# The end of an attention-plus-mixer kernel: last exponentials read from the PSUM banks, values by key tile, softmax sums spread by a matrix product instead of transposed, branch hints on four engines

## The chip, the cores and the metric

One core of one Trainium2 chip runs the whole program. The metric is the device time of one execution in microseconds (us); the median of three runs of the kernel before is 927.33 us (925.99 to 928.0). Engines: PE (TensorE), DVE (VectorE), ACT (ScalarE), POOL (GpSimd) and SP (SyncE, which here issues DMAs and closes the program).

## The reference

The input is one sequence of 2048 tokens with 448 channels. The output mixes two branches with a gate per token: `g * a + (1 - g) * b`, g being the sigmoid of `(x * gate_w).sum(-1)`.

```python
def _A_ref(x, wq, wk, wv, wo):                  # a: 16 query heads of 28, one shared key/value head
    q = (x @ wq).reshape(B, S, H, Dh).transpose(0, 2, 1, 3)
    k = x @ wk
    v = x @ wv
    scores = jnp.einsum("bhqd,bkd->bhqk", q, k) * (Dh ** -0.5)
    p = _softmax(scores, axis=-1)
    o = jnp.einsum("bhqk,bkd->bhqd", p, v)
    return o.transpose(0, 2, 1, 3).reshape(B, S, H * Dh) @ wo
```

Branch b (layer norm, a shifted token mixer, an MLP of width 1792) is finished before the part that this case is about.

## The kernel before, in words

The first 400 us or so project, split matrices into high and low parts, and run branch b; the last 500 us are attention. Attention is 16 units `u` (4 token blocks of 512 by 4 groups of 4 heads), and every unit has 8 stretches `v` of two key tiles of 128 keys each. In a stretch PE makes the scores of 4 heads for two key tiles (L831: three products for each head, into four PSUM banks); `exps` turns a bank into exponentials. Of the four heads, three banks are read by ACT directly (L855, 128x512 each). The fourth (`DRAIN`, head 3) is first copied to SBUF by DVE (L852), and ACT takes both key tiles' copies in one 128x1024 instruction (L860, `late_exps`). The read order of the heads is 0, 3, 1, 2. One stretch later `values` (L871) multiplies the exponentials by `vext`, which holds a column of ones and the 28 value channels: row 32j of the result for head j is the softmax sum. Values go by half of the 512 queries (256 columns), inside a half by key tile; a half's result is added to `o` (128 x 512, L876).

When a unit is done, its sums are fetched from `o` by a small DMA (`sums_begin`, tile `rt`), tested against a limit (`check`, tile `good`), inverted, and sent through DRAM to be spread over 32 partitions (`recip`, tile `rb`); `norm` multiplies, and `wo_job` (L793) multiplies by the output projection, four products side by side in four column groups. DVE then adds the gated result to `ot` (L801), and the output goes out by DMA.

The last unit has no later unit to hide this. Its end before the change is written out (L916 to L996): the sums are added to `o` in four 128x128 pieces (L963), PE transposes `o` (L968) so that the sums lie along the free axis, DVE inverts 8 columns of sums at a time (L931) and multiplies (L935), PE transposes back (L940), ACT copies to SBUF (L941), PE projects (L793), DVE (L951; for token tile 1 ACT L948 and POOL L949) gates and adds, and four DMAs store (L953). Between them `keep_warm` issues bf16 products that nobody reads (L960). The test of the sums ends in one number, `redo`, made from `worst` (L982, then PE L989, DVE L992 and L993). All five engines load `redo` into a register (L996) and branch: if a sum was out of bounds a second, exact pass over all of attention follows (`tc.If`, some thousands of instructions); otherwise they jump over it to the closing instructions (L1071). In the profiled execution the jump is taken. On PE alone `mark_branch_hint_location` puts a hint instruction for that jump in front of the end.

All engines' orders are written by hand (`manual_schedule`): each engine runs its rows in program order, and an instruction that waits holds all that stand behind it on its engine.

## Time and profile before

| what | us |
|---|---|
| median of the runs (3), lowest, highest | 927.33, 925.99, 928.0 |
| the profiled execution | 926.66 |
| its span, first to last instruction | 924.7 |
| PE, ACT, DVE, POOL busy in the span | 911.7, 634.5, 542.2, 104.2 |
| last matmul of the program ends, after about | 917.6 |
| last DVE instruction ends, after about | 918.4 |

Times inside the span count from its first instruction. The 2.0 us between the span and the execution's time lie around the program. Rows of the trace are read as: start, duration, engine, line, operation, written tile <- read tiles, shapes, count, and in brackets the idle time before and what ended it. An engine name with q (SPq, DVEq) is that engine's sequencer: waits, register loads, branches, DMA issues.

### The profile page before, as it was taken

What the parts mean: (1) busy time and instruction counts of PE and PEld (TensorE: products, weight loads), DVE (VectorE), ACT (ScalarE), POOL (GpSimd) and SP (SyncE); (2) the same over time, 40 slices, a digit from 0 to 9 for tenths busy, and PEclk for the clock granted to TensorE, in tenths of its full rate; (3) what the DMA queues carried; (4) which work ended last, traced back from release to release, by engine and by line L of the source; (5) the groups of instructions that cost most, each with busy time, mean ns of one, the idle gap of its engine ahead of it and who ended that gap; (6) DMA issues with size and microseconds to landing.
All of it is one profiled execution on the core that took longest, in us unless ns stands there. A gap on an engine that the chain in (4) does not pass through costs nothing.

```text
span 924.7 us, 23960 instructions
## 1 busy us (share of the span) xinstructions
PE 911.7 (99%) x10051; PEld 647.5 (70%) x10051; DVE 542.2 (59%) x1081; ACT 634.5 (69%) x1134; POOL 104.2 (11%) x135
## 2 busy tenths in 40 slices
PE   9999999999999999999999999999999999999996
PEld 6788888888888888875566666666655656666663
DVE  4665263631435736446666666666666666666664
ACT  5542434432231232259999999999999999999993
POOL 2233200212000440031000000000000000000000
PEclk9999999999999999999999999999999999999999
DMA  9801534130122042110000001001011100110001
GB/s 303 300 27 26 169 128 129 22 84 21 33 65 60 19 104 61 38 54 23 25 23 6 26 14 53 26 26 26 8 41 46 26 4 24 35 45 3 14 14 44
DMA packets 40691, 50.72 MB, mean 55 GB/s; under 512 B 8752, under 2 KB 26880, under 8 KB 40576
## 3 DMA queue, kind: packets, MB, share of 16 engines
q1 hardware_dynamic: 37552, 43.65, 16.4%
q10 hardware_dynamic: 3024, 5.47, 1.6%
q8 instruction: 80, 1.31, 0.6%
q14 instruction: 35, 0.29, 0.1%
HBM read 37.04 MB, written 11.93 MB: 53 GB/s over the span
## 4 chain that ended last, share of the span: by engine, by line
PE 93%; ACT 3%; DMA 2%; DVE 1%; issue 0%; SPq 0%; DVEq 0%; ACTq 0%
PE bank L871 23%; PE bank L831 21%; PE bank L793 7%; PE acc L655 5%; PE acc L654 5%; PE acc L656 5%; PE g L132 4%; PE g L131 4%; PE g L133 4%; ACT p L855 2%; DMA xkv<-in_xT_dram 2%; PE hs L437 1%; PE hs L436 1%; PE hs L438 1%; PE g L135 1%; PE g L134 1%
## 5 line engine op out<-in xcount | busy, mean ns | idle before, releaser
L855 ACT ACTIVATE p<-bank 128x512 f32<-128x512 f32 x768 | 391.0, 626 | 5.8 <-PE bank L831 5.8
L871 PE MATMUL bank<-p,vext 128*32 128x256 f32 x3072 | 243.9, 379 | 2.1 <-ACT p L855 2.1
L871 PE MATMUL bank<-pd,vext 128*32 128x256 f32 x1024 | 242.2, 379 | 0.3 <-ACT pd L860 0.3
L852 DVE COPY pd<-bank 128x512 f32<-128x512 f32 x256 | 176.6, 691 | 53.2 <-PE bank L831 52.3
L871 PEld LDWEIGHTS bank<-p,vext 128*32 128x32 f32 x3072 | 125.1, 110 | 85.8 <-ACT p L855 5.1
L644 ACT ACTIVATE gh<-g 128x512 fp32r<-128x512 f32 x55 | 32.8, 597 | 189.5 <-PE g L135 189.5
L876 DVE TENSOR_TENSOR o<-o,bank 128x256 f32<-128x256 f32 x222 | 93.5, 421 | 91.3 <-ACT p L855 51.0
L860 ACT ACTIVATE pd<-pd 128x1024 f32<-128x1024 f32 x128 | 143.0, 1117 | 0.0
L831 PE MATMUL bank<-qh,kH 30*128 30x512 f32 x1024 | 119.6, 443 | 0.0
L871 PEld LDWEIGHTS bank<-pd,vext 128*32 128x32 f32 x1024 | 111.6, 110 | 1.3 <-ACT pd L860 0.7
L646 DVE TENSOR_TENSOR gl<-gf,gh 128x512 fp32r<-128x512 f32 x55 | 37.9, 690 | 125.5 <-ACT gf L645 125.4
L831 PE MATMUL bank<-qh,kL 28*128 28x512 f32 x1024 | 106.2, 394 | 0.0
L831 PE MATMUL bank<-ql,kH 28*128 28x512 f32 x1024 | 105.7, 389 | 0.0
L831 PEld LDWEIGHTS bank<-qh,kH 30*128 30x128 f32 x1024 | 60.9, 182 | 58.4 <-ACT p L855 47.0
L655 PE MATMUL acc<-w4l,gh 128*128 128x448 f32 x220 | 80.4, 366 | 0.0
L654 PE MATMUL acc<-w4h,gh 128*128 128x448 f32 x220 | 80.3, 365 | 0.0
L656 PE MATMUL acc<-w4h,gl 128*128 128x448 f32 x220 | 80.1, 364 | 0.0
L793 PE MATMUL bank<-wof,on 128*32 128x224 f32 (+1 forms) x992 | 73.1, 370 | 0.3 <-ACT p L855 0.3
L132 PE MATMUL g<-al,w3h 128*128 128x512 f32 x168 | 65.8, 392 | 0.0
L131 PE MATMUL g<-ah,w3h 128*128 128x512 f32 x168 | 65.6, 390 | 0.0
L133 PE MATMUL g<-ah,w3l 128*128 128x512 f32 x168 | 65.5, 390 | 0.0
L831 PEld LDWEIGHTS bank<-ql,kH 28*128 28x128 f32 x1024 | 52.6, 185 | 8.3
(196 smaller groups left out, 1164.8 us busy)
## 6 DMA issues: line engine op xcount, KB each, us to landing
qd<-qf ACTq DMA_DIRECT2D x16, 256.0 KB
qm<-qd SPq DMA_DIRECT2D x16, 256.0 KB
qr<-qd SPq DMA_DIRECT2D x16, 256.0 KB
rb<-rd SPq DMA_DIRECT2D x15, 256.0 KB
x<-in_x_dram SPq DMA_DIRECT2D x4, 896.0 KB
xd<-xt SPq DMA_DIRECT2D x16, 224.0 KB
w34raw<-in_w_dram SPq DMA_DIRECT2D x7, 512.0 KB
out_dram<-ot SPq DMA_DIRECT2D x15, 224.0 KB
```

Of the source, the lines that this page charges most:

```text
L131: nc.tensor.matmul(ps, wh[:, c, :], ah[:, c, :], start=(c == 0), stop=False)
L132: nc.tensor.matmul(ps, wh[:, c, :], al[:, c, :], start=False, stop=False)
L133: nc.tensor.matmul(ps, wl[:, c, :], ah[:, c, :], start=False, stop=False)
L654: nc.tensor.matmul(ps, gh[:, tok], w4h[i][:, k, :], start=(f == 0), stop=False)
L655: nc.tensor.matmul(ps, gh[:, tok], w4l[i][:, k, :], start=False, stop=False)
L656: nc.tensor.matmul(ps, gl[:, tok], w4h[i][:, k, :], start=False, stop=(f == stop))
L793: nc.tensor.matmul(ps[32 * j:32 * j + 32, cols], on_of[u][:, tok], wof[:, g, cols], start=True, stop=True, tile_position=(0, 32 * j))
L831: nc.tensor.matmul(bs[j], w, a, start=(i == 0), stop=(i == 2), tile_position=(32 * j, 0))
L852: nc.vector.tensor_copy(ps[j], bs[j])
L855: behind[kt % 2] = nc.scalar.activation(ps[j], bs[j], AF.Exp, scale=SCALE)
L860: ins = nc.scalar.activation(pd, pd, AF.Exp, scale=SCALE)
L871: nc.tensor.matmul(pv[32 * j:32 * j + 32, q], vext[:, kt, :], p_of[u, kt][j][:, q], start=(kt % 2 == 0), stop=(kt % 2 == 1), tile_position ...
```

## The change

In words:

- The last stretch (`last`) no longer copies head 3's banks; ACT reads all eight banks of the two key tiles, and there is no `late_exps`.
- The last values go by key tile, both halves of key tile 14 and then both of 15; two adds of 128x256 replace four of 128x128.
- The sums are spread by PE: `spread` is a 128x128 matrix whose row 32j holds ones in columns 32j to 32j+31, so that `spread` times `o` puts head j's sum on all its 32 partitions. DVE inverts this result over all columns (128, 128 and 256 of them) and multiplies `o` by it. The transpositions, ACT's copies and the POOL add are gone.
- The test of the last sums goes back to `rt`, fetched by DMA, and stands behind token tile 1's output on DVE. `redo` is now made after the last output instead of before the last two.
- Token tile 3 is projected and stored in two halves of 224 channels. Odd tiles are stored from ACT's queue, even ones from SP's.
- `keep_warm` is called for 2 products in all, instead of 5, 3, 2 and 2.
- The hint stands on PE, DVE, ACT and SP instead of PE alone.
- `spread` is filled by POOL ahead of the attention loop (five memsets).

```diff
-        def exps(u, kt, bs):
+        def exps(u, kt, bs, drain=True):
...
-                if j == DRAIN:
+                if drain and j == DRAIN:
...
+        def value(u, kt, i, pv):
+            q = HALVES[i]
+            for j in range(4):
+                nc.tensor.matmul(pv[32 * j:32 * j + 32, q], vext[:, kt, :], p_of[u, kt][j][:, q],
+                                 start=(kt % 2 == 0), stop=(kt % 2 == 1), tile_position=(0, 32 * j))
...
+            last = k == NU * NV - 1
             for kt in (2 * v, 2 * v + 1):
-                exps(u, kt, scores(u, kt))
-            late_exps(u, v)
+                exps(u, kt, scores(u, kt), not last)
+            if not last:
+                late_exps(u, v)
...
+        pvs = [take(), take()]
+        for kt in (NT - 2, NT - 1):
+            for i in range(2):
+                value(u, kt, i, pvs[i])
+        for i, q in enumerate(HALVES):
+            nc.vector.tensor_add(o[:, q], o[:, q], pvs[i][:, q])
...
+        def spread_sums(i):
+            nc.tensor.matmul(bc[i][:, HALVES[i]], spread, o[:, HALVES[i]], start=True, stop=True)
...
+        def divide(a, b):
+            nc.vector.reciprocal(rb[:, a:b], bc[a // 256][:, a:b])
+            nc.vector.tensor_mul(on_of[u][:, a:b], o[:, a:b], rb[:, a:b])
+
+        def store(n, cols):
+            queue = nc.scalar if n % 2 else nc.sync
+            queue.dma_start(out[0, n * P:(n + 1) * P, cols], ot_of[n][:, cols])
+
+        keep_warm(2)
         with tc.block():
-            tc.mark_branch_hint_location("redo", "LikelyTaken", [mybir.EngineType.PE])
-            keep_warm(5)
-            for t in range(4):
-                nc.tensor.transpose(tp[t // 2][:, t % 2], o[:, toks[t]], ident)
-        keep_warm(3)
-        tail_sums(0)
...
+            tc.mark_branch_hint_location("redo", "LikelyTaken", [
+                mybir.EngineType.PE, mybir.EngineType.DVE, mybir.EngineType.Activation, mybir.EngineType.SP])
+            spread_sums(0)
+        _, _, rt = sums_begin(u, o)
+        spread_sums(1)
+        divide(0, 128)
+        divide(128, 256)
+        divide(256, 512)
+        for t in range(3):
+            wo_job(u, t, send=store)
+            if t == 1:
+                check(rt)
+                worst = s3.tile([P, 1], F32, name="worst")
+                nc.vector.tensor_reduce(worst, good, axis=AX.XY, op=ALU.min)
+        for h in range(2):
+            wo_job(u, 3, slice(224 * h, 224 * h + 224), store)
+        tw = sent[0:1, 0:P]
         nc.tensor.transpose(tw, worst, ident)
         least = s3.tile([1, 1], F32, name="least")
         redo = s3.tile([1, 1], mybir.dt.int32, name="redo")
         nc.vector.tensor_reduce(least, tw, axis=AX.X, op=ALU.min)
         nc.vector.tensor_scalar(redo, least, -1.0, 1.0, op0=ALU.mult, op1=ALU.add)
-        tail_wo(2)
-        tail_wo(3)
         again = nc.values_load(redo, min_val=0, max_val=1)
```

What DVE runs between its last adds to `o` and the load of `redo`, before (line, operation, written tile <- read tiles, columns; numbers behind names are buffers):

```order
L931 RECIPROCAL rr_10955<-bank_3478 128x8
L935 TENSOR_TENSOR on_10956<-bank_3478,rr_10955 128x128 x2
L763 SCALAR_TENSOR_TENSOR good<-bank_3483,good 128x8
L763 SCALAR_TENSOR_TENSOR good<-bank_3478,good 128x8
L982 TENSOR_REDUCE worst<-good 128x1
L951 SCALAR_TENSOR_TENSOR ot_9803<-bank_3483,gg,ot_9803 128x448
L992 TENSOR_REDUCE least<-bank_3481 1x1
L993 TENSOR_SCALAR redo<-least 1x1
L951 SCALAR_TENSOR_TENSOR ot_10033<-bank_3484,gg,ot_10033 128x448
L951 SCALAR_TENSOR_TENSOR ot_10156<-bank_3479,gg,ot_10156 128x448
L996 TENSOR_LOAD redo
```

And the same place of DVE now, from the last reciprocal on (the two ahead of it, with their products, have 128 columns each):

```order
L946 RECIPROCAL rb_10962<-bank_3484 128x256
L947 TENSOR_TENSOR on_10961<-o_10560,rb_10962 128x256
L802 SCALAR_TENSOR_TENSOR ot_9809<-bank_3479,gg,ot_9809 128x448
L802 SCALAR_TENSOR_TENSOR ot_9926<-bank_3482,gg,ot_9926 128x448
L766 SCALAR_TENSOR_TENSOR good<-rt_10971,good 128x16
L968 TENSOR_REDUCE worst<-good 128x1
L802 SCALAR_TENSOR_TENSOR ot_10039<-bank_3485,gg,ot_10039 128x448
L802 SCALAR_TENSOR_TENSOR ot_10162<-bank_3480,gg,ot_10162 128x224
L802 SCALAR_TENSOR_TENSOR ot_10162<-bank_3483,gg,ot_10162 128x224
L975 TENSOR_REDUCE least<-bank_3478 1x1
L976 TENSOR_SCALAR redo<-least 1x1
L977 TENSOR_LOAD redo
```

All four token tiles' outputs now stand behind the last reciprocal, and `redo` has moved from between the outputs to the very end.

What ACT runs from its last two exponentials to the branch, before:

```order
L855 ACTIVATE p_3505<-bank_3478 128x512
L860 ACTIVATE pd_3513<-pd_3513 128x1024
L964 UNCONDITIONAL_BRANCH x2
L941 COPY on_10954<-bank_3481 128x128
L941 COPY on_10954<-bank_3484 128x128
L941 COPY on_10954<-bank_3479 128x128
L941 COPY on_10954<-bank_3482 128x128
L948 ACTIVATE y<-bank_3478,gg 128x448
L953 DMA out_dram<-ot_9920 128x448
L996 TENSOR_LOAD redo
L999 COMPARE_AND_BRANCH
```

And now:

```order
L858 ACTIVATE p_3512<-bank_3483 128x512
L858 ACTIVATE p_3513<-bank_3478 128x512
L954 UNCONDITIONAL_BRANCH
L1052 BRANCH_PREFETCH_HINT
L954 UNCONDITIONAL_BRANCH
L951 DMA out_dram<-ot_9926 128x448
L951 DMA out_dram<-ot_10162 128x224 x2
L977 TENSOR_LOAD redo
L980 COMPARE_AND_BRANCH
```

ACT has two 128x512 exponentials in place of one 128x1024, then only a hint and three DMA issues up to the branch; DVE and SP have the same hint at the same place of the program.

More of the change, by code (lines that the diff above doesn't have):

```diff
@@ L756, in gated_mix_kernel, with check @@
         on_of = {}
-        good = s3.tile([P, 8, 4], F32, name="good")
+        good = s3.tile([P, 4, 4], F32, name="good")
         nc.gpsimd.memset(good, 1.0)
-        def check(sums, c):
-            g = good[:, c:c + sums.shape[1]]
-            nc.vector.scalar_tensor_tensor(g, sums, LIMIT, g, op0=ALU.is_le, op1=ALU.min)
+        spread = s3.tile([P, P], F32, name="spread")
+        nc.gpsimd.memset(spread, 0.0)
+        for j in range(4):
+            nc.gpsimd.memset(spread[32 * j:32 * j + 1, 32 * j:32 * j + 32], 1.0)
+        def check(rt):
+            nc.vector.scalar_tensor_tensor(good, rt.rearrange("p (a b) -> p a b", b=4), LIMIT, good,
+                                           op0=ALU.is_le, op1=ALU.min)
         def sums_begin(u, o):
@@ L785, in gated_mix_kernel, with wo_job @@
         ot_of = {}
-        def wo_job(u, t, end=None, cols=slice(0, D)):
+        def wo_job(u, t, cols=slice(0, D), send=None):
             b, g = divmod(u, NG)
```

97 lines of the change are left out of this document (23 added, 74 removed).

## The prediction

> **What bounds the kernel now.** I read the page first, for whether any engine but PE matters.
>
> ```profile
> span 924.7 us, 23960 instructions
> PE 911.7 (99%) x10051; PEld 647.5 (70%) x10051; DVE 542.2 (59%) x1081; ACT 634.5 (69%) x1134; POOL 104.2 (11%) x135
> ```
>
> PE is busy almost throughout, and the change leaves its 900 us of loops as they are. POOL's five extra memsets stand ahead of the attention loop on an engine that is busy for 11%; behind them it weighs four tiles that PE's fifth stretch needs, so four stretches hide them, and they would cost some tenths if not. The question is the last 20 us. The chain of waits, asked for that stretch (start, duration, what), ends with the last output add:
>
> ```profile
> 902.31 1.73 PE bank L871 x32
> ...
> 908.02 0.94 ACT pd L860
> ...
> 909.01 1.91 PE bank L871 x26
> ...
> 917.69 0.68 DVE ot L951
> ```
>
> That is at 918.4, and the span ends at 924.7: 6.3 us are neither matmul nor vector work. The branch to the end and its closing lines fill them (durations in ns, then first and last start in us):
>
> ```profile
> L999 SPq EVENT_SEMAPHORE  x8: 17/17/17, 922.8 to 923.3; - x8
> L999 POOLq COMPARE_BRANCH  x1: 45/45/45, 917.1 to 917.1; - x1
> L999 PEldq COMPARE_BRANCH  x1: 998/998/998, 917.1 to 917.1; - x1
> L999 POOLq EVENT_SEMAPHORE  x1: 17/17/17, 917.7 to 917.7; - x1
> L999 PEldq EVENT_SEMAPHORE  x1: 51/51/51, 918.2 to 918.2; - x1
> L999 DVEq COMPARE_BRANCH  x1: 72/72/72, 918.4 to 918.4; - x1
> L999 ACTq COMPARE_BRANCH  x1: 54/54/54, 918.7 to 918.7; - x1
> L999 SPq COMPARE_BRANCH  x1: 45/45/45, 919.9 to 919.9; - x1
> L999 DVEq EVENT_SEMAPHORE  x1: 21/21/21, 922.2 to 922.2; - x1
> L999 ACTq EVENT_SEMAPHORE  x1: 17/17/17, 922.6 to 922.6; - x1
> ```
>
> ```profile
> L1071 PEldq BRANCH_PREFETCH_HINT  x1: 45/45/45, 909.1 to 909.1; - x1
> ```
>
> From its branch to its next instruction PE, the one engine with a hint, needs 1.1 us and POOL 0.6, but DVE 3.8, ACT 3.9 and SP 2.9. SP is last, and from there its closing waits take 1.9 us to the end of the span (922.8 to 924.7). A table by stretches shows what runs meanwhile (last three columns: granted PE clock, share of the DMA engines, GB/s), and the DMA view from 917.6 on counts the packets that carry instructions (packets, MB, share):
>
> ```profile
> 918.50:920.40 1.90, 0.00 (x0) 0.00 (x0) 0.00 (x0) 0.00 (x0) 0.00 (x0) 1.00 0.98 353
> 920.40:922.30 1.90, 0.00 (x0) 0.00 (x0) 0.00 (x0) 0.00 (x0) 0.00 (x0) 1.00 0.11 31
> ```
>
> ```profile
> q14 instruction: 6, 0.05, 2.2%
> q8 instruction: 1, 0.02, 1.0%
> ```
>
> The outputs fill the DMA engines until 920.4; a remainder drips on until 922.3, beside some of seven instruction fetches. So **two things end at nearly the same time**: SP's branch (922.8) and the last output (about 922.3).
>
> **The change, term by term.** Durations first (busy us, mean ns of one):
>
> ```profile
> L774 DVE RECIPROCAL rr<-rt 128x16 f32<-128x16 f32 x15 | 3.7, 246 | 0.0
> L763 DVE SCALAR_TENSOR_TENSOR good<-rt,good 128x16 f32<-128x16 f32 x15 | 2.5, 166 | 0.0
> ```
>
> ```profile
> L876 DVE TENSOR_TENSOR o<-o,bank 128x256 f32<-128x256 f32 x5 | 2.1, 421 | 2.1 <-PE bank L871 1.3 <-ACT p L855 0.8
> L951 DVE SCALAR_TENSOR_TENSOR ot<-bank,gg,ot 128x448 f32<-128x448 f32 x3 | 2.1, 684 | 1.5 <-PE bank L793 1.5
> L801 DVE SCALAR_TENSOR_TENSOR ot<-bank,gg,ot 128x224 f32<-128x224 f32 x4 | 1.6, 441 | 0.0
> L935 DVE TENSOR_TENSOR on<-bank,rr 128x128 f32<-128x128 f32 x4 | 1.0, 286 | 0.1
> L931 DVE RECIPROCAL rr<-bank 128x8 f32<-128x8 f32 x2 | 0.4, 204 | 0.5 <-PE bank L968 0.5
> L992 DVE TENSOR_REDUCE least<-bank 1x1 f32<-1x128 f32 x1 | 0.3, 279 | 0.7 <-PE bank L989 0.7
> L763 DVE SCALAR_TENSOR_TENSOR good<-bank,good 128x8 f32<-128x8 f32 x2 | 0.2, 156 | 0.0
> ```
>
> ```profile
> 904.98 3.04 ACT L855 ACTIVATE p<-bank 128x512 f32<-128x512 f32 x6 [0.30 <-PE bank L831]
> ```
>
> ```profile
> 911.90 0.21 DVE L931 RECIPROCAL rr<-bank 128x8 f32<-128x8 f32 x1 [0.45 <-PE bank L968]
> 912.14 0.49 DVE L935 TENSOR_TENSOR on<-bank,rr 128x128 f32<-128x128 f32 x2
> ...
> 912.78 0.49 DVE L935 TENSOR_TENSOR on<-bank,rr 128x128 f32<-128x128 f32 x2
> ...
> 916.33 0.14 DVE L993 TENSOR_SCALAR redo<-least 1x1 int32<-1x1 f32 x1
> ```
>
> *Exponentials and values.* Six exponentials in 3.04 us are 0.48 us apart, so eight end at 904.98 + 7 x 0.48 + 0.62 = 909.0, where the 1024-wide one ended too (908.96): no gain on ACT. But key tile 14 is then multiplied already, and behind the last exponential stand the products of key tile 15 alone, 16 of 32 records: 0.87 us instead of 1.91. I give 0.3 of this back, since the values of the stretch before get their first bank only from the third exponential instead of the second, and PE then runs without a stall. PE ends at about 910.2 instead of 910.9. DVE's second add (0.42) ends at 910.7.
>
> *Spread.* The first `spread` product runs behind the first add: two passes of 256 columns, about 0.7 us by the L871 rate (1.73 us for 8 rounds of passes) plus the filling of the array. The first reciprocal starts at about 911.1, before it was 911.9. Up to here **-0.8 us**.
>
> *Reciprocals.* The trace has none wide. From 8 to 16 columns the time grows by 42 ns, 5.25 ns a column, on 162 ns fixed; the check (156 and 166 ns) grows by 1.3 ns a column. So 128 columns take 0.83 us and 256 take 1.51. Ends: at plain speed (L935) 0.29 and 0.42, 2.2 us less in all; if everything that 8 columns cost over the 156 - 8 = 148 ns of a plain operation is per column, 7.0 ns, so 0.86 us more in all. The low end is out, since 16 columns already cost 80 ns over a check of 16. I take 5.25, from the reciprocals themselves, and keep 5.25 to 7.0. Each multiplication starts 0.04 behind, and the next instruction 0.21 behind its start (L935, two in 0.49). Two pieces of 1.08, then 1.51 + 0.04 + 0.42: the last piece ends at 915.2. Before, all four were multiplied by 913.3. The gain of 0.8 has become a loss.
>
> *Page against row.* The Trainium skill (VectorE: DVE Perf Modes, First, the fixed hardware budget) says that Reciprocal is an iterated divide with a repeat count of 8. At one repeat per plain column time (421 - 286 over 128 columns, 1.05 ns) an estimate by it is 8.4 ns a column, 1.6 us more in all. The 16-column row speaks against that: 16 x 8.4 + 148 is 282 ns, and it took 246.
>
> *Outputs and flag.* All on DVE now, in order: 448 columns 0.60 apart, twice; check and `worst` 0.3; 0.60; the two halves 0.36 each and 0.1 for a second wait. PE stays ahead: its projections run from 915.3, 0.4 us a pass of 448 columns (two passes of 256 in 0.43 by the L871 rate, and 448/256 of that), and are done by about 917.2. The last output is added at 918.1 (918.4 before). `least` and `redo`: 0.28 + 0.14, so **the flag is there at 918.5, before at 916.5**. What hid it, two outputs, is gone. The sums' DMA is issued on SP at 910.7, five us ahead of SP's next issue; the check that waits for it stands at 916.3 with `worst` and two tiles' outputs behind it, so it is hidden unless it takes over five us. The dropped warm-up products cost nothing while the clock stays up: the windows above grant 1.00 until 922.3, over four us after the last matmul, and PE's longest new gap is about one.
>
> *Branches.* Behind the flag stand five register loads and branches:
>
> ```profile
> L996 DVEq TENSOR_LOAD <-redo x1: 543/543/543, 917.7 to 917.7; - x1
> ...
> L996 SPq TENSOR_LOAD <-redo x1: 763/763/763, 918.8 to 918.8; - x1
> ```
>
> DVE, ACT and PE branch at 919.1; SP needs 1.1 us from load to branch (918.8 to 919.9) and does so at 919.7. A branch whose target is already in the engine costs 0.6 (POOL) to 1.1 us (PE); with 0.6 SP goes on at 920.3 and ends 1.9 later, at 922.2. The last output is issued at 918.2; by the rows above the bulk lands 2.0 to 2.4 us after its issue, 920.5, just in time for SP's waits (0.5 us into them); with a remainder as before (3.9 us) 922.1, and the end is 923.5. Fewer fetches stand beside it now, so I take an end of 922.6: **2.1 us less** than 924.7. Without hints, the same flag gives: DVE 922.9, ACT 923.0, SP 922.6, end 924.5 to 924.9.
>
> The sum is therefore 926.66 - 2.1 = 924.6 against the profiled execution. Its time lies 0.67 under the median; against the median the forecast is **925.2 us**.
>
> **Rivals.**
>
> *The hints do not take (927.3).* For it, PE's own hint: executed at 909.1, and yet no packet moved until 915.5; PE's only fetch (queue q8) between hint and branch is in the window 915.5 to 917.0; the third row is that queue's count in the whole span.
>
> ```profile
> DMA packets 0, 0.00 MB, mean 0 GB/s; under 512 B 0, under 2 KB 0, under 8 KB 0
> ```
>
> ```profile
> q8 instruction: 1, 0.02, 4.4%
> ```
>
> ```profile
> q8 instruction: 80, 1.31, 0.6%
> ```
>
> So a hint did not fetch at once; it acted some 100 PE instructions later, near the branch. If it acts when the program steps into its next block (20102 PE instructions against 80 fetches on q8, some 250 a block), DVE, ACT and SP, with a handful to 17 rows between hint and branch, will mostly not step into one, and PE, whose end is shorter now, may not either. Against it: PE did find its target. Then the end is the 924.5 to 924.9 above: no change. The Trainium skill (Runtime: NRT & Kernel Launch, Instruction fetch mechanics) holds prefetch to be purely sequential and a taken branch out of the window to force a fetch; the trace agrees on DVE, ACT and SP, not on hinted PE.
>
> *Slower: the late flag behind dear reciprocals (928.2).* Place: DVE, 911 to 915. At 7.0 ns a column the flag comes at 919.4, and with no hint taking, all branches 0.9 later than in the rival above: end 925.6. Without hints it decides from about 5.5 ns on; for 0.2% it would take 9 ns. With hints it still ends at 923.5.
>
> *The values do not gain (925.9).* If PE waits for ACT's last two exponentials in both halves as it did for the pairs, the 0.7 us go back, hints taking.
>
> **How the numbers follow.** Hints take and values gain, 0.55: 925.2, with 924.1 to 926.4 by the branch (0.3 to 1.1), the remainder of the output and 5.25 to 7.0 ns. Hints do not take, 0.30: 927.3, 926.8 to 928.0. Values do not gain, 0.05: 925.9. Dear reciprocals and no hints, 0.10: 928.2 and beyond. The range is 924.1 to 928.0. A measurement tells about 0.2% from no change, 1.9 us, so under 925.5 is faster: 0.42, three quarters of the first case and a little of the others. Within: 0.51. Slower, over 929.2: 0.07, the upper part of the last case with the output's remainder on top.
>
> **What would show it.** Right: the first reciprocal near 911.1, 0.8 and 1.5 us long; the flag near 918.5; SP from branch to next instruction under 1.2 us; no instruction fetch between the branches and the closing waits. Wrong: 3 us or more from a branch to the next instruction on DVE, ACT or SP; wide reciprocals near 0.3 us (then the time falls under 924) or over 1.1 us; SP's closing waits held by the last output.

## The result and the profile after

The changed kernel takes 929.78 us (median of 20 runs, 927.80 to 931.38); the kernel before, measured beside it, 927.78 us (median of 20, 925.42 to 929.36). The ratio is **1.0020, with a 95% interval of 1.0013 to 1.0027**: slower by 1.2 to 2.5 us. The forecast was 925.2, with a range from 924.1 to 928.0. The profiled execution of after took 928.07 us with a span of 926.3, against 926.66 and 924.7 before.

The chain of waits of after, from its last values on (start, duration, what):

```profile
907.18 3.56 PE bank L869 x64
...
911.65 0.97 DVE rb L946
...
916.31 1.72 PE bank L797 x24
...
919.26 0.14 DVE redo L976
```

The last stretch starts 0.49 us later in this execution than in that of before (904.46 against 903.97, timeline rows below). Where a time of after is compared with a forecast below, these 0.49 are taken off and it is said so. The last values are one piece now, 64 products without a stall. From the first reciprocal on DVE works almost without a gap up to the flag; from 916.3 to 918.2 the chain goes over PE's last projections and its transposition of `worst`, beside which DVE adds the first outputs. It ends with the flag, no longer with an output.

The two shapes of the reciprocal (busy us, mean ns of one | idle time before):

```profile
L946 DVE RECIPROCAL rb<-bank 128x128 f32<-128x128 f32 x2 | 1.9, 954 | 0.4 <-PE bank L941 0.4
L946 DVE RECIPROCAL rb<-bank 128x256 f32<-128x256 f32 x1 | 1.7, 1749 | 0.0
```

Between the two shapes lie 795 ns for 128 columns: 6.2 ns a column.

The register load of the flag on DVE, and the branches behind the five loads (ns, then first and last start):

```profile
L977 DVEq TENSOR_LOAD <-redo x1: 761/761/761, 919.4 to 919.4; - x1
```

```profile
L980 SPq EVENT_SEMAPHORE  x8: 17/17/17, 924.3 to 924.9; - x8
...
L980 ACTq COMPARE_BRANCH  x1: 68/68/68, 920.3 to 920.3; - x1
L980 DVEq COMPARE_BRANCH  x1: 84/84/84, 920.3 to 920.3; - x1
L980 PEldq COMPARE_BRANCH  x1: 430/430/430, 920.3 to 920.3; - x1
L980 SPq COMPARE_BRANCH  x1: 70/70/70, 920.5 to 920.5; - x1
...
L980 PEldq EVENT_SEMAPHORE  x1: 51/51/51, 920.8 to 920.8; - x1
L980 ACTq EVENT_SEMAPHORE  x1: 17/17/17, 924.1 to 924.1; - x1
L980 DVEq EVENT_SEMAPHORE  x1: 21/21/21, 924.2 to 924.2; - x1
```

From branch to next instruction ACT needs 3.8 us, DVE 3.9, SP 3.8, PE 0.5. So **the three added hints saved nothing**; SP even needs 0.9 us more than before (2.9). The hints were executed:

```profile
L1052 SPq BRANCH_PREFETCH_HINT  x1: 65/65/65, 886.8 to 886.8; - x1
L1052 ACTq BRANCH_PREFETCH_HINT  x1: 50/50/50, 906.3 to 906.3; - x1
L1052 DVEq BRANCH_PREFETCH_HINT  x1: 56/56/56, 910.9 to 910.9; - x1
```

The DMA view of after counts instruction packets (packets, MB, share). By the number and the places of their packets, queue q8 serves PE (16 KB each) and q14 the other engines (8 KB each). The window 887.5 to 920.5, from just behind SP's hint to the branches, has a row for q8 and none for q14; the window behind the branches, 920.5 to 924, has both:

```profile
q8 instruction: 4, 0.07, 0.8%
```

```profile
q14 instruction: 4, 0.03, 3.1%
q8 instruction: 1, 0.02, 2.1%
```

The four packets of q14 start between 921.2 and 921.6, while the three engines go on at 924.1 to 924.3; what fills the time in between is not shown.

A second loss is not in the tail at all. The first scores of the 34th stretch of 128 (the expectations call it the 33rd, counting from 0) and of the last one stand in the timelines of before and of after (start, duration, engine, line) at:

```profile
537.11 0.51 PE L831 MATMUL bank<-qh,kH 30*128 30x512 f32 x4
903.97 0.50 PE L831 MATMUL bank<-qh,kH 30*128 30x512 f32 x4
```

```profile
536.90 0.51 PE L834 MATMUL bank<-qh,kH 30*128 30x512 f32 x4
904.46 0.51 PE L834 MATMUL bank<-qh,kH 30*128 30x512 f32 x4
```

The same stretches of the loop take 366.86 us before and 367.56 after. I call this difference the **loop** of a run, and the time from the last stretch's first scores to the end of the span its **tail**: 20.8 us before (924.7 - 903.97), 21.8 after (926.3 - 904.46). Both are read in this way from every run's one profile. The tail grew by 1.0 us, the loop by 0.7. Nearly all of the 1.0 is SP's longer way behind its branch: counted from the last stretch's first scores, SP branches at 16.1 us (before 16.0) and goes on at 19.9 (before 18.8).

### The profile page after: what moved, and what is told of

It reads as the page before. It is cut to its first block, busy times and chain, and to the rows that moved or that the text cites. A ratio compares the mean times of both kernels' runs of the same rounds, so it can differ in the third digit from the quotient of the medians.

```text
span 926.3 us, 23945 instructions
## 1 busy us (share of the span) xinstructions
PE 910.8 (98%) x10045; PEld 645.6 (70%) x10045; DVE 544.6 (59%) x1078; ACT 633.8 (68%) x1130; POOL 103.2 (11%) x139
## 3 DMA queue, kind: packets, MB, share of 16 engines
q1 hardware_dynamic: 37540, 43.43, 16.1%
## 4 chain that ended last, share of the span: by engine, by line
PE 95%; ACT 2%; DVE 1%; DMA 1%; issue 0%; ACTq 0%
PE bank L869 23%; PE bank L834 21%; PE bank L797 7%; PE acc L655 5%; PE acc L654 5%; PE acc L656 5%; PE g L132 4%; PE g L131 4%; PE g L133 4%; ACT p L858 2%; PE hs L437 1%; PE hs L436 1%; PE hs L438 1%; PE g L135 1%; PE g L134 1%; PE h L131 1%
```

## The experiments

Times are ratios to the kernel before on the same chip, with 95% intervals. "Early hints" are DVE's and ACT's hints in the first stretch of the last but one unit and SP's in that of the ninth.

| run | ratio | interval | tail, us | loop, us |
|---|---|---|---|---|
| before | 1 | | 20.8 | 366.86 |
| changed | 1.0020 | 1.0013 to 1.0027 | 21.8 | 367.56 |
| e1 changed, PE's hint alone | 1.0016 | 1.0007 to 1.0025 | 22.1 | 367.4 |
| e2 changed, early hints | 0.9980 | 0.9971 to 0.9990 | 18.5 | 367.4 |
| e10 changed, two steps early | 0.9982 | 0.9973 to 0.9991 | 18.6 | 367.5 |
| e15 changed, behind the step | 1.0002 | 0.9992 to 1.0011 | 21.1 | 367.3 |
| e3 before, early hints | 0.9995 | 0.9987 to 1.0004 | 20.3 | 367.0 |
| e4 before, values by key tile | 0.9988 | 0.9971 to 1.0006 | 19.9 | 366.9 |
| e7 before, values, early hints | 1.0000 | 0.9980 to 1.0020 | 20.0 | 367.0 |
| e12 the same, flag before the last output | 0.9984 | 0.9974 to 0.9993 | 19.7 | 367.0 |
| e8 the same, flag last | 0.9958 | 0.9944 to 0.9971 | 17.5 | 367.0 |
| e11 before, flag last | 0.9995 | 0.9986 to 1.0004 | 20.5 | 367.0 |
| e6 changed, early hints, early flag | 1.0006 | 0.9997 to 1.0015 | 20.9 | 367.6 |
| e9 the same, PE not held | 1.0006 | 0.9997 to 1.0015 | 20.5 | 367.4 |
| e5 changed, no division | 0.9983 | 0.9974 to 0.9991 | 19.5 | 367.6 |
| e13 before, tiles shifted | 1.0010 | 1.0000 to 1.0020 | 20.9 | 367.6 |
| e14 changed, tiles of before | 1.0013 | 1.0003 to 1.0022 | 22.1 | 366.8 |

### Where a hint has to stand: e1, e2, e10, e15

The theory was that a hint acts when its engine steps into a further block of instructions, and that the three added hints stand behind the last such step. The rivals were that hints act on PE alone, and that a hint only needs some microseconds of lead. e1 takes the three hints out:

```diff
-            tc.mark_branch_hint_location("redo", "LikelyTaken", [
-                mybir.EngineType.PE, mybir.EngineType.DVE, mybir.EngineType.Activation, mybir.EngineType.SP])
+            tc.mark_branch_hint_location("redo", "LikelyTaken", [mybir.EngineType.PE])
```

> The changed kernel with the hint on PE alone; nothing else differs. Theory of the late hint (the three added hints stand behind the last block of instructions that their engines fetch before the branch, so they do nothing): from branch to next instruction 3.8 to 3.9 us on DVE and ACT and 2.9 to 3.8 on SP, span 925.5 to 926.5, time within 0.2% of the changed kernel (1.000 to 1.004 of before). Rival, a hint that does not take does harm (SP's way from branch to next instruction went from 2.9 us before to 3.8 after): SP needs 2.9 again, and the end is 0.9 us earlier, 928.9 us or 1.001 of before. Second rival, the hints saved something that something else ate: 1 us slower, 1.003 or more.

Measured: 1.0016, not to be told from the changed kernel, and 4.1 to 4.2 us from branch to next instruction on DVE, ACT and SP. The hints did neither good nor harm, and SP's longer way is not their doing.

e2 moves the three hints up:

```diff
+        HINT_AT = {64: [mybir.EngineType.SP], 112: [mybir.EngineType.DVE, mybir.EngineType.Activation]}
+
         for k in range(NU * NV):
...
+            if k in HINT_AT:
+                with tc.block():
+                    tc.mark_branch_hint_location("redo", "LikelyTaken", HINT_AT[k])
+                    exps(u, 2 * v, scores(u, 2 * v), not last)
...
```

> The changed kernel, with DVE's and ACT's hints moved to the first stretch of the last but one unit (about 840 us) and SP's to the first stretch of the ninth (about 636 us): each then stands ahead of that engine's last fetch of instructions (877.4, 871.0 and 684.0 us in the trace after). PE's hint stays where it is. Theory of the late hint: a hint acts when its engine steps into its next block, so all three targets are fetched there; from branch to next instruction 0.5 to 1.1 us on DVE, ACT and SP in place of 3.8 to 3.9, no instruction fetch between 920 and 923 except the ones that follow the target, and the span ends 2.7 to 3.3 us earlier (SP's branch at 920.5, plus 0.6, plus 1.9 for the closing waits: 923.0; the last output has landed at 921.0 and holds nothing): 926.5 to 927.1 us, 0.9986 to 0.9993 of before. Rival, hints act on PE alone: 3.8 to 3.9 us as in the changed kernel, time within 0.2% of it. Second rival, a target fetched that early is thrown out or takes the place of the block that follows: a stall of about 3.8 us in the loop at the next step (871 to 877 us), time the same or up to 3 us more.

Measured: 0.9980, 925.06 us. The rows of e2 (two of the hints, then branches and what follows them):

```profile
L1057 SPq BRANCH_PREFETCH_HINT  x1: 65/65/65, 638.6 to 638.6; - x1
L1057 DVEq BRANCH_PREFETCH_HINT  x1: 56/56/56, 845.5 to 845.5; - x1
```

```profile
L985 SPq EVENT_SEMAPHORE  x8: 17/17/17, 921.4 to 921.9; - x8
...
L985 DVEq COMPARE_BRANCH  x1: 84/84/84, 920.5 to 920.5; - x1
...
L985 SPq COMPARE_BRANCH  x1: 70/70/70, 920.8 to 920.8; - x1
...
L985 DVEq EVENT_SEMAPHORE  x1: 21/21/21, 921.2 to 921.2; - x1
```

DVE goes on 0.62 us behind its branch, SP 0.54 (the rows are rounded). The tail shrinks from 21.8 to 18.5 us. One edit of place turns the change from slower into faster.

e15 tells the step from the lead: DVE's and ACT's hints stand some 30 us ahead of their branches, but behind their last step. Its edit is 112 turned into 123.

> The changed kernel with SP's hint early as before (about 636 us), and DVE's and ACT's in the fourth stretch of the last unit (about 888 us): some 30 us ahead of their branches, but behind their last fetches of instructions (871 and 877 us). Theory that a hint acts only when its engine steps into its next block: DVE and ACT need 3.8 us from branch to next instruction as in the changed kernel, SP 0.6; no fetch on q14 between 888 and 920; the end waits for DVE and ACT, 1.001 to 1.0025 of before. Rival, a hint only needs some microseconds of lead: all three in 0.5 to 0.7 us and 0.998 as with the early hints.

```profile
L1057 DVEq BRANCH_PREFETCH_HINT  x1: 56/56/56, 888.9 to 888.9; - x1
```

```profile
L985 SPq EVENT_SEMAPHORE  x8: 17/17/17, 922.0 to 922.6; - x8
...
L985 DVEq COMPARE_BRANCH  x1: 84/84/84, 921.2 to 921.2; - x1
...
L985 SPq COMPARE_BRANCH  x1: 70/70/70, 921.5 to 921.5; - x1
...
L985 DVEq EVENT_SEMAPHORE  x1: 21/21/21, 925.4 to 925.4; - x1
```

In one and the same run SP, with its hint ahead of its last step, goes on after 0.5 us, and DVE, with 32 us of lead but no step left, after 4.2. The rival of the lead time is out. The last two fetches on q14 ahead of the branches (ACT's and DVE's) lie in the window 865 to 885, and none lies between the hints and the branches:

```profile
q14 instruction: 2, 0.02, 0.3%
```

The time was some 0.1% better than the theory expected: with SP already waiting, the end came about 1 us behind DVE's and ACT's next instructions (925.4, span 926.5) and not 1.9.

e10 puts DVE's and ACT's hints eight stretches earlier again (112 turned into 104), ahead of two steps.

> The changed kernel with early hints, but DVE's and ACT's hints eight stretches earlier again (first stretch of the third last unit, about 806 us), so that two of their fetches follow it and not one: DVE's at about 817.6 and 877.4 us, ACT's at 820.5 and 871.0. Theory that one hint changes one fetch (the block at the next step is the target in place of the one that follows in order): the next block in order is then missing at the second step, so DVE and ACT stall about 3.8 us at 871 to 877 us, PE behind them stands for 2 to 4 us, and the branch may miss as well: 2 to 6 us more than the early hints, 1.000 to 1.004 of before, with an extra fetch on q14 at 871 to 877. Rival, the hint is kept until its branch: 0.998 as with the early hints, one fetch at each step, and 0.5 to 0.7 us from branch to next instruction. Second rival, the target is fetched at the first step, thrown out by the second: no stall in the loop, but 3.8 us at the branch, 1.0015 as the changed kernel.

Measured: 0.9982 and a tail of 18.6 us, as e2, with no stall in the loop (367.5). My theory that a hint spends itself on the next step falls; the first rival holds. A hint is kept, over at least one step, until it is of use: here the hints ran at 814.0 and 815.5 us, and q14 fetched at 819 and 822 and again at 873 and 879. What fits all four runs is that a hint acts at the step into the block that holds the branch. The counts of q14 over the whole span, in the changed kernel and then in e2, say a little more:

```profile
q14 instruction: 36, 0.29, 0.1%
```

```profile
q14 instruction: 33, 0.27, 0.1%
```

Ahead of the branches q14 makes the same number of fetches in both, and in e1, e10 and e15 too: 29 between 40 and 900 us. Behind them it makes 7 in the changed kernel and in e1, 4 in e2 and e10, and 6 in e15, where SP alone is hit. So a hint that works saves a fetch behind the branch and adds none ahead of it. That the last fetch ahead of the branch brings the branch's target in place of the block that follows in order is the simplest reading; what a packet holds no trace shows. The Trainium skill (Runtime: NRT & Kernel Launch, Instruction fetch mechanics) calls prefetch purely sequential and says that a taken branch out of the window forces a fetch. The rows of after agree for the three engines whose hint came too late; e2 and e10 show that a hint ahead of the last step gets round it.

### The flag and the last output: e3, e7, e8, e12, e11

e3 gives the kernel before the same early hints.

> The kernel before, with hints for DVE, ACT and SP added at the same early places (first stretch of the ninth and of the last but one unit); its end is otherwise as before. Theory of the late hint: DVE, ACT and SP go on 0.5 to 1.1 us after their branches (918.4, 918.7, 919.9), so SP at 920.5. What ends last is then the last output, which landed at 922.3 to 922.7 in the trace before. If the late remainder of that output came from the instruction fetches beside it, it lands at about 921 and the span ends 1.9 us after SP's 920.5, at 922.4: 2.3 us less, 0.9975 of before. If it did not, SP's closing waits stand until 922.7 and the end moves by 0.3 us at most: 0.9997, the same. Rival, hints act on PE alone: 3.8, 3.9 and 2.9 us again, 1.000.

```profile
L1005 SPq EVENT_SEMAPHORE  x8: 17/17/17, 921.9 to 924.4; - x8
...
L1005 SPq COMPARE_BRANCH  x1: 70/70/70, 921.4 to 921.4; - x1
```

The hints took (SP goes on after 0.5 us), and the time is the same, 0.9995. SP's eight closing waits, which take 0.5 us where nothing holds them, now stand 2.5 us for the last output. That output's late remainder is still there although no branch missed. For a hit does not spare all fetches: the blocks behind the target follow, and the window 921.7 to 924 of e3 has

```profile
q14 instruction: 3, 0.02, 3.4%
q8 instruction: 1, 0.02, 2.6%
```

So the next question was whether an early branch harms the outputs. e7, e12 and e8 are one kernel (before's tail, values by key tile, early hints) with `least` and `redo` at three places: early as before, ahead of the last output's add, and behind it. The edit of e8 against e7:

```diff
-        tw = bank("worst_t")[0:1, 0:P]
...
-        nc.vector.tensor_scalar(redo, least, -1.0, 1.0, op0=ALU.mult, op1=ALU.add)
         tail_wo(2)
         tail_wo(3)
+        tw = bank("worst_t")[0:1, 0:P]
...
+        nc.vector.tensor_scalar(redo, least, -1.0, 1.0, op0=ALU.mult, op1=ALU.add)
```

> The kernel before with two parts together: all eight exponentials of the last stretch by ACT with the values multiplied key tile by key tile, and early hints on DVE, ACT and SP. Its tail and its early flag are before's. Theory (the last output sets the end, as the instruction fetches behind the early branches share its engines): the hints are worth nothing here and the values 0.6 us: 0.9985 to 0.9993 of before, and the last output lands 3.5 us or more behind its issue. Rival, the parts help one another: the outputs are 0.7 us earlier and the branches too, end 2 us earlier, 0.9975.

> As the kernel with the values by key tile, early hints and before's tail, but with the flag computed last: the transposition of worst, least and redo stand behind the last output's add. In the frame of the trace before: last output added at 917.7, flag at 918.2, branches of DVE, ACT and PE at 918.8 and of SP at 919.1 to 919.4. Theory that fetches behind the branches hold up outputs still in flight: the fetches now come at 920, when the last output has landed (2.0 to 2.4 us behind its issue, 919.9), so the end is SP's 919.7 plus 1.9, 921.6 to 922: 2.7 to 3.1 us less than before, 0.9967 to 0.9972, and faster than the same kernel with the early flag although the flag comes over 2 us later. Rival, an early flag is always as good or better: at or above the kernel with the early flag, 0.998 to 1.000.

> As the fastest so far (before's tail, values by key tile, early hints, flag last), but least and redo stand ahead of the last output's add and not behind it. The flag comes 0.6 us earlier, the last output 0.4 us later. Theory of the fetches: PE's and POOL's branches and their fetches meet the last output in flight, which lands 2.5 us or more behind its add, and the time is 0.4 to 1.5 us more than with the flag last: 0.9965 to 0.998 of before. Rival, the flag is still the bound there: 0.2 to 0.4 us less, 0.9953.

Measured: 1.0000, 0.9984 and 0.9958, with tails of 20.0, 19.7 and 17.5 us: **with the flag behind the last output the end comes over 2 us sooner**, although the flag itself comes later. e7 and e12 cannot be told apart by their times. SP's closing waits in e7, then in e8:

```profile
L1011 SPq EVENT_SEMAPHORE  x8: 17/17/17, 920.1 to 922.9; - x8
```

```profile
L1011 SPq EVENT_SEMAPHORE  x8: 17/17/17, 921.2 to 921.7; - x8
```

And a table by stretches of e7 (the last three columns: granted PE clock, share of the DMA engines, GB/s):

```profile
920.50:921.50 1.00, 0.00 (x0) 0.00 (x0) 0.00 (x0) 0.00 (x0) 0.00 (x0) 1.00 0.09 15
921.50:922.50 1.00, 0.00 (x0) 0.00 (x0) 0.00 (x0) 0.00 (x0) 0.00 (x0) 0.82 0.04 11
```

The remainder drips at a share of 0.04 to 0.09, about one DMA engine of sixteen (0.06), while SP waits for it. Seven runs with an early flag have a remainder like this (before, e3, e4, e7, e9, e12, e13): the last packet lands 3.6 to 4.4 us behind the last output's add. None with a late one has it (changed, e1, e2, e5, e8, e10, e11, e14, e15: 1.6 to 2.1 us); e6, below, is a case of its own. That the flag's place makes it is shown. That it is done by an instruction packet in front of the output's packets on one engine is argued, and e12 comes nearest to showing it. Two of its DMA windows, 919.2 to 919.3 and 921 to 922, have these rows among others:

```profile
q8 instruction: 1, 0.02, 109.6%
```

```profile
q1 hardware_dynamic: 9, 0.01, 6.4%
```

The packet for PE takes 109.6% of 16 engines' 0.1 us, 1.75 us, and so lasts to about 921.0. From 920.05 to 921 no packet of the output moves. Then nine follow on q1, the queue of SP's stores, at about the share of one engine in sixteen, and the output has landed. No run moves such a fetch by itself.

e8, at 924.08 us (median of 6), is the fastest kernel of this study, ahead of both before and the changed kernel. e12's forecast was for 0.9965 to 0.998; it came out a little worse. e7's time says little for itself (its interval is 0.4% wide), but its tail agrees with its rows.

e11 moves the flag of the kernel before in the same way and adds no hint.

> The kernel before, with one thing moved: worst's transposition, least and redo stand behind the last output's add. No hint is added, and exponentials and values are as before. It prices the late flag by itself. Last output added at 918.4 as before, flag at 918.8 in place of 916.5; branches at 919.4, SP's at 919.7 to 920.0. Theory: without hints SP, DVE and ACT need 2.9 to 3.9 us from there, so SP goes on at 923.3 to 923.8 and the span ends 0.5 to 1.0 us later than before, 925.2 to 925.7: 1.0005 to 1.001; the last output lands at 920.8 without its late remainder. Rival, undisturbed outputs bring more than the late flag costs: 0.999. Second rival, the flag is worth its whole 2.3 us: 1.0025.

Measured: 0.9995, tail 20.5 against 20.8.

```profile
L999 SPq EVENT_SEMAPHORE  x8: 17/17/17, 922.0 to 922.6; - x8
...
L999 SPq COMPARE_BRANCH  x1: 45/45/45, 919.2 to 919.2; - x1
```

My expectation of 0.5 to 1.0 us more fell: the flag came later by some two microseconds and cost nothing. The outputs were undisturbed, but that is not the reason, for in before the remainder (until 922.2) was over when SP went on (922.8). The reason is SP, whose closing waits end the program. Its register load stands behind its issue of the last output, so in before it loads at 918.8 a flag that has been there since 916.5. Counted from the last stretch's first scores, in e11 DVE ends the last output's add 0.35 us earlier than in before, as `least` and `redo` no longer stand ahead of it, and SP goes on at 18.6 us against 18.8.

### The flag in the changed tail: e6, e9

e6 computes the flag early in the changed tail, with the early hints.

```diff
+        check(rt)
+        worst = s3.tile([P, 1], F32, name="worst")
+        nc.vector.tensor_reduce(worst, good, axis=AX.XY, op=ALU.min)
         for t in range(3):
             wo_job(u, t, send=store)
+            if t == 0:
...
+                nc.tensor.transpose(tw, worst, ident)
...
+                nc.vector.tensor_reduce(least, tw, axis=AX.X, op=ALU.min)
+                nc.vector.tensor_scalar(redo, least, -1.0, 1.0, op0=ALU.mult, op1=ALU.add)
```

> The changed kernel with the early hints, and its flag computed early: check and worst behind the third multiplication, worst's transposition behind the first output's projection, least and redo behind the first output's add. DVE has the same instructions, in another order. Flag at about 917.7 in the frame of the trace after (919.4 there), last output added at about 919.45 (919.04 there); PE and POOL branch at about 918.3, with the outputs still to be sent. Theory that the instruction fetches that follow a branch (one of 16 KB and three or four of 8 KB, also where the hint took) hold up the outputs beside them: the last output lands at 922 to 923.5, 2.5 us or more behind its issue, and the span ends at 923.3 to 924.5, no gain over the early hints with the late flag (923.3), 0.998 to 0.999 of before. Rival, the late flag is what sets the end and the outputs are not disturbed: landing at 921.4, end at about 922.8, 0.5 us less than with the late flag.

The run gave 1.0006 but does not answer the question, since another thing happened. PE's rows (last, in brackets, the idle time before), and the clock that was granted:

```profile
917.97 0.37 PE L975 MATMUL bank<-ident,worst 128*1 128x128 f32 x1 [2.65 <-DVE worst L970]
918.27 4.71 PE L797 MATMUL bank<-wof,on 128*32 128x448 f32 x32
```

```profile
915.00:916.00 1.00, 0.32 (x4) 0.00 (x0) 0.97 (x3) 0.00 (x0) 0.00 (x0) 1.00 0.00 0
...
917.00:918.00 1.00, 0.03 (x1) 0.03 (x1) 0.93 (x5) 0.00 (x0) 0.00 (x0) 0.50 0.00 0
```

PE stood 2.65 us for `worst` with the second projection queued behind it. Its clock fell to a half, and the projections took 4.7 us. e9 mends that: the transposition stands behind the second projection, and the clock stays at 1.00.

> As the changed kernel with early hints and the early flag, but with worst's transposition behind the second projection in place of the first, and least and redo behind the second output's add. In the run with the first order PE stood 2.65 us for worst with the second projection behind it, its granted clock fell from 1.00 to 0.50 and the remaining projections took 4.7 us, which hid what was asked. Now PE waits no longer than in the changed kernel (about 1.2 us), so the clock should stay at 1.00 and the projections behind the transposition take 1.7 us. Theory of the fetches: flag about 1.3 us earlier than in the changed kernel, last output added 0.4 later; PE's and POOL's branches and their fetches now fall beside the outputs; last output lands 2.4 us or more behind its add (1.9 in the changed kernel with early hints), so no gain over the early hints with the late flag: 0.998 to 0.9995 of before. Rival, an earlier flag is a gain once PE is not held: 0.5 us less than with the late flag, 0.997 to 0.9975.

Measured: 1.0006, tail 20.5 against the 18.5 of e2. The early flag costs two microseconds in the changed tail too, more than expected. 0.4 of them are the last output's add, which now stands behind the flag; the rest is its remainder, which lands 3.6 us behind the add, against 1.6 in e2.

### Values by key tile, and the reciprocals: e4, e5

e4 gives before the new exponentials and values alone (`exps(..., drain)` and the loop by key tile, as in the change).

> The kernel before with one part of the change alone: in the last stretch all eight exponentials are read from the banks by ACT, and the last values are multiplied key tile by key tile. The tail of before stands behind it. Theory (step one of the forecast): ACT's last exponential ends where it did, PE's last value product ends 0.6 to 0.7 us earlier (910.2 in place of 910.9, against the same start of the last stretch), the outputs follow 0.6 earlier and the flag too, and the time falls by 0.4 to 0.7 us: 0.9993 to 0.9996. Rival, the eight exponentials end later than the 1024 wide one did, or the stretch before stalls for its bank: no gain, 1.000 to 1.0005. Second rival, the last output's remainder sets the end whatever the branches do: products 0.6 earlier and time unchanged.

```profile
909.62 1.73 PE bank L921 x32
```

The values end at 911.35 in a run whose last stretch started 1.10 us later than that of before (905.07 against 903.97). In before's frame that is 910.25, 0.67 us earlier than the 910.92 there. The time, 0.9988, agrees, but its interval reaches over 1.

e5 replaces the reciprocals by copies, so it multiplies by the sums where the reference divides by them:

```diff
-            nc.vector.reciprocal(rb[:, a:b], bc[a // 256][:, a:b])
+            nc.vector.tensor_copy(rb[:, a:b], bc[a // 256][:, a:b])
```

> The changed kernel (its hints as they are), with the three reciprocals of the tail replaced by plain copies of the same columns from the same banks, so that the last unit's values are multiplied by their sums and not divided by them; nothing else differs. It prices the reciprocals in place. The trace after has 0.96, 0.95 and 1.75 us for 128, 128 and 256 columns, 6.2 ns a column; plain passes over 128 and 256 columns took 0.29 and 0.42 us before. Theory that the reciprocals stand on the path to the flag, DVE being without a gap from 911.7 to 919.4: the flag comes 2.4 to 2.7 us earlier and so does the end, 927.1 to 927.4 us, 0.9994 to 0.9998 of before. If PE's last projections take over as the limit, 1.5 to 2 us. Rival, the reciprocals are hidden: unchanged, 1.002.

Measured: 0.9983, tail 19.5 against 21.8 and 22.1 (changed and e1): 2.3 to 2.6 us. The reciprocals stand on the path to the flag with nearly all that they cost over copies (3.66 against 0.99 us).

### The loop: e13, e14

The difference of 0.7 us in the loop came back in every kernel with the changed tail. The new table for the spread pushes every tile of the attention loop 448 bytes up. e13 does only that to the kernel before; e14 undoes it in the changed kernel (the table is allocated behind the loop, 64 bytes fill the gap).

```diff
+        pad = s3.tile([P, 112], F32, name="pad")
+        nc.gpsimd.memset(pad, 0.0)
```

> The kernel before with one tile of 448 bytes per partition, written once and never read, put in where the changed kernel has its table for the spread: every tile of the attention loop then lies at the changed kernel's address, and nothing else differs. The traces so far show the loop from its 33rd to its last stretch at 366.9 to 367.0 us in all kernels with before's tail and at 367.4 to 367.6 in all with the changed tail, some 6 ns more in nearly every stretch from the 14th on. Theory that the addresses do it: 367.4 to 367.6 here, and the time 0.5 us more, 1.0003 to 1.0008. Rival, something else of the change (the check's form, the order of the code) does it: 366.9 to 367.0 and 1.000.

> The changed kernel with the spread table allocated and written behind the attention loop, and 64 bytes put in behind the smaller check tile, so that the loop's tiles lie at the addresses of before. Theory that the addresses cost the 0.5 us in the loop: 33rd to last stretch 366.9 to 367.0 us in place of 367.4 to 367.6, and the time 0.5 us less than the changed kernel, 1.0011 to 1.0018 of before. Rival: 367.4 to 367.6 as in the changed kernel, 1.002.

The 34th and the last stretch in e13, then in e14:

```profile
537.46 0.51 PE L833 MATMUL bank<-qh,kH 30*128 30x512 f32 x4
905.04 0.51 PE L833 MATMUL bank<-qh,kH 30*128 30x512 f32 x4
```

```profile
537.63 0.51 PE L832 MATMUL bank<-qh,kH 30*128 30x512 f32 x4
904.46 0.50 PE L832 MATMUL bank<-qh,kH 30*128 30x512 f32 x4
```

The shift alone gives 367.58 us; taking it out gives 366.83. **The addresses cost the 0.7 us** (0.3 to 0.8 by the other runs of the table), 3 to 8 ns in each of 94 stretches. The times by themselves would not settle it, for the interval of e13 reaches down to 1.0000 and that of e14 overlaps the changed kernel's; the loops do: the eight kernels with before's addresses have 366.8 to 367.0, the nine with the shifted ones 367.3 to 367.6. Which tile's address it is stays open. e13's first 32 stretches took 1.2 us more than in the other runs of its kind, in its one profile; that is not explained.

## Why the prediction was wrong, step by step

**Exponentials and values: right.** Forecast 910.2 for PE's last value product; measured 910.74, less the 0.49 by which this execution's stretch starts later: 910.25. e4 gives the same.

**Spread: right.** First reciprocal forecast at 911.1, measured 911.65 - 0.49 = 911.16.

**Reciprocals: mis-sized.** I took 5.25 ns a column, from two rows of 8 and 16 columns, and kept 7.0 as the other end; the runs showed 6.2. The three took 3.66 us in place of 3.17, 0.5 us more; e5 shows that nearly all of it counts. The Trainium skill's repeat count of 8 (VectorE: DVE Perf Modes, First, the fixed hardware budget), 8.4 ns by the forecast's estimate, was 2.2 ns above, more than twice as far as the slope of the narrow rows was below.

**Flag and branches: late by 0.7.** The flag came at 919.40 - 0.49 = 918.9 for a forecast of 918.5 (the reciprocals), and DVE's branch at 919.8 for 919.1: five register loads at nearly the same moment took 0.59 to 0.76 us and DVE's branch 0.1 more, where I had allowed 0.6 together.

**Hints: the step that failed.** I let the hints bring the target into the engine, so that SP goes on 0.6 us behind its branch, and gave this 0.55. It took 3.8. The rival "The hints do not take" named the condition that e2, e10 and e15 have since borne out, a step into the next block, and found that DVE, ACT and SP would mostly have none between hint and branch. I gave it 0.30, held against it that PE did find its target, and did not follow it up, though q14's fetches in the trace of before would have settled it: the last two ahead of the branches start at 870.5 and 876.9 us, and the added hints ran at 886.8 (SP), 906.3 (ACT) and 910.9 (DVE). e2, which has the hints where they act, came out at 925.06 us with a tail 2.2 us shorter than before's, where the forecast had 925.2 and 2.1. So the sum was about right under a condition that did not hold. That it agrees to 0.1 us is partly luck: less the 0.78 us by which its last stretch starts later than before's, SP branched 0.4 us later than forecast, and the 0.4 that I had kept for a remainder of the last output was not needed; the loop's 0.5 us, which the forecast lacks, is hidden by the spread between executions.

**The case without hints: also too low.** For it I had 927.3 us, and 928.2 with dearer reciprocals; measured 929.8. The second comes nearer, the rival with 0.10: at 6.2 ns a column the reciprocals lie above the 5.5 from which I let the flag decide. Of the gap of 2.5 to 927.3 about 1.1 us lie in the tail: less the 0.49, the span ends at 925.8, where I had 924.5 to 924.9. SP branches 0.4 late (reciprocals, loads), and then needs 3.8 us where I had taken over its 2.9 from before; a little of this was covered, as I let the end come 1.9 us behind ACT's next instruction too, where e15 has about 1. About 0.5 is the later start of the last stretch, out of the loop. The last 1.0 is spread between executions: the profiled one of after lies 1.7 under its median (928.07 against 929.78) where that of before lies 1.1 under its own (926.66 against 927.78), and the median of before was 0.45 higher beside the changed kernel than when the forecast was made (927.33).

**The loop: a term that was missing.** I wrote that the change "leaves its 900 us of loops as they are". It does in their instructions, not in their addresses: 0.7 us (e13, e14).

**The late flag: priced with the wrong sign.** I counted the loss of "what hid it, two outputs" as a cost, and took the last output's remainder for something that fewer fetches would shrink. e3, e7 and e12 showed it with all hints hit; e8 and e11 that a flag behind the outputs removes it. So the late flag by itself was no loss (e11). Nor is the changed kernel's 1.0 us of longer tail on the path to the flag: the values' 0.7, the transpositions and copies that are gone, and the 2.3 to 2.6 us of reciprocals over plain passes (e5) come out even to 0.1 us at SP's branch. The other 0.9 is SP's miss, 3.8 us in place of 2.9. It takes 3.8 to 4.1 us in the changed kernel, e1, e5 and e14, and 2.6 to 2.9 in before, e4, e11 and e13. The added hints are not the cause (e1); what is stays open.

## What to carry to other kernels

A branch hint is worth its 3 us only if its engine still fetches a block of instructions behind it: count the fetches on the instruction queue between the hint's place and the branch, per engine, and put the hint ahead of the last. Do not branch while the last outputs are in flight: in these runs a flag ahead of the last output's landing cost that output 2 us, hit or miss, most likely by the fetches behind the branch; it costs time where the output, and not the branch, ends the program. A new table allocated ahead of a loop's tiles can slow the loop without touching one of its instructions; allocate it behind them.

## What the runs showed of the hardware

A hint was kept over a step of its engine into a new block and still worked (e10, 106 us and more ahead of its branch). A wide reciprocal costs 6.2 ns a column on 128 partitions, with about 0.16 us fixed. PE's granted clock fell to 0.50 in a run where PE waited 2.65 us (e6), and it stayed at 1.00 over a gap of 1.2 us in the changed kernel. The Trainium skill (TensorE: Matmul & The Clock Gate, What's actually happening) gives about 3.4 us of idleness in a free-running window; here a shorter gap, behind a microsecond in which PE was busy for 0.32, was enough. A shift of 448 bytes in a loop's tiles changed its time by 0.2%.
